# A fused attention and token-mixing kernel: w2 loaded in 11 pieces, matmul pairs with their own waits, all gate logits on VectorE, and another order of all tasks

## The chip, the core and the metric

The kernel runs on one core of a Trainium2 chip. The metric is the device time of one execution in microseconds (us), as the median of several runs. A core has five engines that run side by side, each through its own queue in order: PE (TensorE, matrix products into PSUM), ACT (ScalarE), DVE (VectorE), POOL (GpSimd) and SP (SyncE, which here only issues DMAs). They wait for each other through semaphores.

## What is computed

Two mixers work on the same x, of 2048 tokens by 512 features in bf16, and a gate mixes their results. A is attention with 32 heads of 16 features, in which a token sees itself and the 255 before it. B is a layer norm followed by a two-layer perceptron across tokens: its first product sums over the 2048 tokens (w1, 2048 x 1376), its second goes back to them (w2, 1376 x 2048).

```
g = sigmoid((x * gate_w).sum(-1))
a = softmax(mask(q @ k.T) * 16 ** -0.5) @ v @ wo       # q, k, v = x @ wqkv, per head
b = (gelu(layernorm(x).T @ w1 + b1) @ w2 + b2).T
out = g * a + (1 - g) * b
```

## The kernel before

Everything is resident in SBUF. Tokens are cut into 16 tiles of 128; group i means four tiles, 512 tokens. The program is a list of tasks, made by `add`. Each has a name, the engines that may do it, the tasks it depends on, and the buffers it takes. Two texts then fix the order: `PLAN` (from line 190) names for each engine the tasks in the order of its queue, with the numbers of the buffers each takes after the colon, and `THEN` names those attention tasks after which a plain matmul task is issued in column tiles. `arrange` (line 85) steps through these queues with estimated costs. It no longer chooses the order in a queue; it settles how the queues are interleaved when the program is written out, and which of the shared-port waits are set between VectorE and GpSimd. So `PLAN` and `THEN` set what runs; the costs in `arrange` served to search them.

The tasks that matter here, by name:

- `x0.0`, `x1.4` and so on: loads of x. `wqk0` to `wqk3`, `wv`: loads of wqkv. `xt1` to `xt3`: transposing loads of x by DMA (line 463); group 0 is transposed on TensorE (`xta`) and copied (`xtc`). `gw`: gate_w copied to all partitions. `w1_gi`: a quarter (512 tokens) of a group g of w1's columns. `w2_g`: w2, in the old kernel in 3 tasks of 4, 4 and 3 chunks of 128 rows. w2 lies in the same memory as w1, so a piece of it can be loaded only when the matmuls that read that part of w1 are done.
- `q`, `k`, `v`: projections, in chains of 4 matmuls (`chain`, line 653; its matmul is line 670). `qc`, `kc`, `vc` copy them out of PSUM. `vs` and `vz` move parts of V to other partitions by DMA (lines 718 to 729); `vz` has 3 buffers.
- For each block j of 128 queries, shifted by 64: `sj.v0` to `sj.v3` and `sj.C` are scores on TensorE (lines 942, 998, 1042); `e...` the exponentials on ScalarE (line 894); `m...` the masks, on VectorE (lines 907, 974) or GpSimd (line 536); `pvj` the products with V (line 1087); `n1j` to `n4j` and `nzj` the transposition and division on VectorE (lines 1178 to 1213). The result is put over x.
- `bs`, `ba`, `pow`, `h`: layer norm. `u0` to `u10`: 11 chains of 16 matmuls over tokens, one for 128 columns of w1; `ub` adds the bias; `gelu` acts on all of them.
- `gate0` with `gatem0`: gate logits of group 0 by 16 matmuls of one column (line 802); `gl4` to `gl15`: those of the other tiles on VectorE, one fused multiply-and-sum each (line 822). `gatee` and `ez` make the exponentials and spread them.
- `y0` to `y15`: for each output tile a chain of 11 matmuls with w2 and 4 with wo, in pairs; `f` scales and adds on the way out of PSUM (lines 438, 441), `o` stores (line 1305). `y15` is made in two halves of 256 columns, `y15l` and `y15r`.

A chain is issued in pieces of two matmuls, so that others can stand between; `u3.4` is the piece that begins with matmul 4. In the old kernel the first piece of a `u` chain waits for all four quarters of its group of w1 and all 16 `h`, and the first piece of a `y` chain for all of w2. TensorE has modes: plain 128 x 128 work ("d"), column tiles ("p"), scores ("s"), corners ("c", "h"). A change between them has a price, for which `arrange` has `SWITCH`. PSUM has 8 banks; a task on TensorE that takes a bank waits until the last reader of it is done.

Of the kernel before, what the change touches and what calls it, by code (L numbers as in the profile page):

```python
# [78 lines left out]
SWITCH = 0.095  # L79

BLOCK, AHEAD, FETCH, BUSY = 256, 80, 3.6, 3.0
LATENCY = {"PE": 0.22, "ACT": 0.15, "DVE": 0.12, "POOL": 0.15, "SP": 2.0}


def arrange(tasks):
# [19 lines left out]
    count, come, loads = AHEAD, {}, 0.0  # L105
    order = []
    while len(order) < len(tasks):
# [117 lines left out]
    ACT="""
        xtc0.0.1 xtc0.1.0 xtc0.1.1 kc3_0 kc1_0 kc0_0 kc2_0 e0.v0.0:4 e0.v0.1:5 kc3_1 e0.C.1:8 e0.C.0:a e-1.C.1:7
        e-1.C.0:b vc1 vc2 e1.v3.1:2 e1.v3.0:3 vc3 e1.v0.0:6 e1.v0.1:9 vc5 gatee0 e0.v1.0:d e0.v1.1:c vc14 kc2_1
        vc13 e1.v2.1:b e1.v2.0:7 vc12 vc15 kc2_2 e1.v1.0:5 e1.v1.1:a vc4 e2.v1.1:4 e2.v1.0:8 e1.C.1:d e1.C.0:c vc7
# [42 lines left out]
    """,  # L271
    SP="""
        x0.0 x0.2 wqk0 wqk1 wqk2 wqk3 x1.4 xt1 wv x2.8 bias xt3 x3.12 xt2 vs0 w1_02 w1_03 vs1 w1_22 vs2 gw w1_12
        w1_23 w1_01 w1_00 w1_10 w1_11 vz2:0 w1_13 vz3:1 vz4:2 vz5:0 w1_20 w1_21 vz6:1 vz8:0 w2_0 vz7:2 w2_1 w2_2
        vz9:1 wo o0 o4 o8 o7 vz10:2 vs13 o2 o9 o1 vz11:0 vz12:1 o5 o10 vz13:2 o11 vz14:0 o3 o6 o12 o14 o13 o15l
        o15r
    """,
# [1097 lines left out]
```

## Time and profile before

| | |
|---|---|
| Median of 3 runs | 199.59 us (198.86 to 199.63) |
| Profiled execution | 199.82 us, of which the span from first to last instruction is 198.1 |
| TensorE clock granted | 1.000 |
| Matmuls | 4058 |
| ACT, exponentials (lines with L894) | 89.3 + 58.1 us in two groups |
| GpSimd, masks (L536) | 46.7 + 20.0 us in two groups |
| DMA | 22.02 MB, 111 GB/s on average |

The page counts busy time for each engine, in total and in 40 slices, follows the chain of waits back from the end, and lists groups of instructions with their mean length and what ended the idle time ahead of them. Time is counted from the start of the span. The "end" of a matmul is modelled, so I go by starts: the next start less this one is what a matmul costs the stream. The DMA loads that matter:

```profile
wb<-in_B_w_dram SPq DMA_DIRECT2D x8, 512.0 KB, 8.2
wb<-in_B_w_dram SPq DMA_DIRECT2D x2, 2048.0 KB, 9.2
VZ<-VA SPq DMA_DIRECT2D x26, 70.0 KB, 3.0
xo<-in_A_x_dram SPq DMA_DIRECT2D x3, 512.0 KB, 5.5
```

The last number is the median from issue to landing in us. `wb` holds w1 and later w2.

### The profile page before, as it was taken

The numbers are of one execution on the slowest core, as the hardware profiler recorded it, in microseconds if no ns is written. First come the engines' busy times: TensorE is split into PE (matmuls) and PEld (weight loads), VectorE is DVE, ScalarE is ACT, GpSimd is POOL, SyncE is SP. The second block draws the span as 40 slices with busy tenths as digits, with TensorE's granted clock in tenths as the row PEclk, the third lists the DMA queues.
The fourth block names the chain that finished last, engine by engine and source line by source line (L and its number), as shares of the span: only waits on it lengthen the run. The fifth ranks groups of instructions, "written<-read, shape, count | busy, mean of one in ns | idle before, by whom it ended". The sixth has DMA issues, their size and how long they took to land. (4 is left out here: it accounts for less than half of the span.)

```text
span 198.1 us, 9100 instructions
## 1 busy us (share of the span) xinstructions
PE 193.0 (97%) x4058; PEld 93.3 (47%) x4058; DVE 156.5 (79%) x318; ACT 169.0 (85%) x198; POOL 80.0 (40%) x118
## 2 busy tenths in 40 slices
PE   7999999999999999999999999999999999999993
PEld 3643444353635445446543554344445354554572
DVE  1799888879998988986589799636867868869683
ACT  2369999999988996998999899899899989898632
POOL 6394897525344440214223200045069335452310
PEclk9999999999999999999999999999999999999999
DMA  5999798970060000001399770000211220200002
GB/s 156 294 284 232 131 319 278 346 187 0 8 174 18 18 0 3 3 5 32 98 364 367 280 210 3 26 26 30 68 37 58 60 68 22 62 30 30 30 3 83
DMA packets 23189, 22.02 MB, mean 111 GB/s; under 512 B 7566, under 2 KB 21262, under 8 KB 23150
## 3 DMA queue, kind: packets, MB, share of 16 engines
q1 hardware_dynamic: 23150, 21.44, 36.9%
q8 instruction: 32, 0.52, 1.1%
q14 instruction: 7, 0.06, 0.1%
HBM read 15.61 MB, written 2.10 MB: 89 GB/s over the span
## 5 line engine op out<-in xcount | busy, mean ns | idle before, releaser
L894 ACT ACTIVATE et<-ps 128x1024 bf16<-128x1024 f32 (+1 forms) x94 | 89.3, 1015 | 6.1 <-PE ps L942 2.4
L536 POOL TENSOR_SCALAR_AFFINE_SELECT et<-et 128x512 bf16<-128x512 bf16 (+2 forms) x63 | 46.7, 751 | 56.0 <-ACT et L894 40.9
L894 ACT ACTIVATE XT<-ps 128x1024 bf16<-128x1024 f32 (+1 forms) x60 | 58.1, 1011 | 7.3 <-PE ps L942 4.3
L670 PEld LDWEIGHTS <-wb 128*32 128x32 bf16 (+4 forms) x645 | 32.0, 97 | 34.5 <-issue 6.5
L670 PE MATMUL pb<-ug,wb 128*32 128x512 bf16 (+4 forms) x385 | 45.5, 366 | 0.0
L670 PE MATMUL pb<-h,wb 128*128 128x512 bf16 (+2 forms) x260 | 44.5, 381 | 0.0
L536 POOL TENSOR_SCALAR_AFFINE_SELECT XT<-XT 128x512 bf16<-128x512 bf16 (+1 forms) x28 | 20.0, 720 | 46.3 <-ACT XT L894 27.4
L670 PE MATMUL pb<-XT,wqkv 128*128 128x512 bf16 (+2 forms) x190 | 32.4, 372 | 0.4 <-DMA wqkv<-in_A_wqkv_dram 0.3
L1178 DVE STREAM_TRANSPOSE et<-ps 128x1024 f32<-128x1024 f32 (+1 forms) x17 | 20.1, 1183 | 11.9 <-PE ps L1087 11.1
L1087 PEld LDWEIGHTS <-VA 128*32 128x32 bf16 (+1 forms) x1056 | 20.1, 97 | 6.6 <-issue 1.5
L942 PE MATMUL ps<-QZ,KT 32*128 32x256 bf16 (+1 forms) x496 | 23.1, 265 | 0.0
L754 DVE TENSOR_TENSOR QZ<-pb,par 128x1024 bf16<-128x1024 f32 x16 | 19.5, 1221 | 3.2 <-PE pb L670 3.2
L670 PEld LDWEIGHTS <-wqkv 128*128 128x128 bf16 (+1 forms) x190 | 12.7, 98 | 14.6 <-DMA wqkv<-in_A_wqkv_dram 0.5
L670 PE MATMUL pb<-wo,xo 128*32 128x512 bf16 (+2 forms) x152 | 18.1, 375 | 0.0
L1087 PE MATMUL ps<-et,VA 128*32 128x128 bf16 (+2 forms) x624 | 17.9, 218 | 0.0
L942 PEld LDWEIGHTS <-KT 32*128 32x128 bf16 x496 | 7.4, 92 | 20.6 <-ACT et L894 10.7
L670 PE MATMUL pb<-wqkv,XT 128*128 128x512 bf16 (+1 forms) x70 | 16.5, 381 | 0.0
L974 DVE TENSOR_TENSOR et<-et,mask 128x512 bf16<-128x512 bf16 x26 | 13.3, 510 | 2.5 <-ACT et L894 2.4
L441 DVE TENSOR_SCALAR ot<-pb,c,c 128x512 bf16<-128x512 f32 (+1 forms) x11 | 8.6, 785 | 7.4 <-PE pb L670 7.3
L1087 PE MATMUL ps<-XT,VA 128*32 128x128 bf16 (+2 forms) x432 | 13.9, 215 | 0.0
L1087 PEld LDWEIGHTS <-VZ 128*32 128x32 bf16 x832 | 13.2, 98 | 0.7
L770 DVE BATCH_NORM_STATS2 stats<-xo 128x6 f32<-128x512 bf16 x16 | 10.7, 682 | 3.1 <-DMA xo<-in_A_x_dram 3.1
(76 smaller groups left out, 199.4 us busy)
## 6 DMA issues: line engine op xcount, KB each, us to landing
wb<-in_B_w_dram SPq DMA_DIRECT2D x8, 512.0 KB, 8.2
wb<-in_B_w_dram SPq DMA_DIRECT2D x2, 2048.0 KB, 9.2
VZ<-VA SPq DMA_DIRECT2D x26, 70.0 KB, 3.0
xo<-in_A_x_dram SPq DMA_DIRECT2D x3, 512.0 KB, 5.5
out_dram<-ot SPq DMA_DIRECT2D x12, 128.0 KB, 2.4
wb<-in_B_w_dram SPq DMA_DIRECT2D x4, 352.0 KB, 5.8
wqkv<-in_A_wqkv_dram SPq DMA_DIRECT2D x4, 256.0 KB, 5.0
wb<-in_B_w_dram SPq DMA_DIRECT2D x1, 1024.0 KB, 5.3
```

Of the source, the lines that this page charges most:

```text
L441: return nc.vector.tensor_scalar(out=out_, in0=in_, scalar1=scale, scalar2=bias, op0=ALU.mult, op1=ALU.add)
L536: return nc.gpsimd.affine_select(out=out_, in_=in_, pattern=[[0, n] for n in pattern] + [[step, HB]], compare_op=op, fill=0.0, base=base_, ...
L670: made.append(nc.tensor.matmul(buf(b)[c:z_, c0:c0 + w_], lhsT=lhsT[:, c:z_], rhs=rhs, start=(j == 0), stop=(j == n - 1), skip_group_check= ...
L754: lambda k=k, b=b: nc.vector.tensor_tensor(out=QZ[:, k, :, (i % NQ) * SB:(i % NQ + 1) * SB], in0=buf(b)[:, None, :].to_broadcast([P, 2, SB ...
L770: f"bs{t_}", {"DVE": 0.67}, lambda b=b, t_=t_: nc.vector.bn_stats(buf(b)[:], xo[:, t_, :]),
L894: lambda e=e, b=b, shape=shape: nc.scalar.activation(out=shape(buf(e)), in_=shape(buf(b)), func=ACT.Exp, scale=SCALE),
L942: made.append(nc.tensor.matmul(to[:, :, done:done + m], lhsT=keys(j if x == "A" else j - 1, k)[rows], rhs=q[rows], start=True, stop=True, ...
L974: made.append(nc.vector.tensor_tensor(out=v, in0=v, in1=m.to_broadcast(list(v.shape)), op=ALU.mult))
L1087: return lambda: nc.tensor.matmul(to(), lhsT=v() if callable(v) else v, rhs=buf(e)[rows, col:col + n], start=first, stop=last, tile_positi ...
L1178: lambda: nc.vector.transpose(out=view(buf(tr).bitcast(FP32)), in_=view(buf(o))), [last], takes=[tr], uses=[o],
```

## The change

It does five things.

1. `PLAN` and `THEN` are new for all engines. They were searched with other costs: a table `TURN` of the price of each change of mode, `cost_of` for tasks, other hand-over times, and a finer account of when TensorE's instructions are fetched and of loads that compete with it.
2. w2 is loaded in 11 pieces, one for each chunk of 128 rows (`w2_0` to `w2_10`), each waiting only for the u matmuls that read the part of w1 beneath it.
3. Pairs wait for their own pieces: in `u` for a quarter of w1 and one `h` per matmul, in `y` for one piece of w2.
4. `NGP = 0`: the logits of group 0 go to VectorE too (`gl0` to `gl3`), and `gate0` is gone.
5. `y15` is made in three parts, of 256, 128 and 128 columns (`y15l`, `y15m`, `y15r`). The zeros for the warm-up matmuls are 128 columns in place of 512 and read repeatedly.

Which engine does a task changes with `PLAN`: masks go from GpSimd to VectorE (GpSimd 82 to 67, VectorE 70 to 85). On VectorE `kc` goes from 7 to 5, `vc` from 2 to 5, `ub` from 7 to 5, `f` from 14 to 13, `xtc` from 1 to 2; ScalarE has the others.

```diff
-SWITCH = 0.095
-
-BLOCK, AHEAD, FETCH, BUSY = 256, 80, 3.6, 3.0
-LATENCY = {"PE": 0.22, "ACT": 0.15, "DVE": 0.12, "POOL": 0.15, "SP": 2.0}
+TURN = {
+    "d": dict(d=0, s=0.100, p=0.100, c=0.098, h=0.100),
...
+BLOCK, AHEAD, INSIDE, FETCH, BUSY = 256, 77, 194, 4.0, 2.4
+LATENCY = {"PE": 0.21, "ACT": 0.15, "DVE": 0.11, "POOL": 0.12, "SP": 2.3}
+
+
+def cost_of(t, e):
+    c, n = t.engines[e], t.name
+    if e == "PE":
+        return c - 0.02 if t.mode == "s" else c * 0.738 if t.mode == "c" else c
+    if e == "DVE":
+        return max(0.1, c - 0.06)
...
     SP="""
-        x0.0 x0.2 wqk0 wqk1 wqk2 wqk3 x1.4 xt1 wv x2.8 bias xt3 x3.12 xt2 vs0 w1_02 w1_03 vs1 w1_22 vs2 gw w1_12
-        w1_23 w1_01 w1_00 w1_10 w1_11 vz2:0 w1_13 vz3:1 vz4:2 vz5:0 w1_20 w1_21 vz6:1 vz8:0 w2_0 vz7:2 w2_1 w2_2
-        vz9:1 wo o0 o4 o8 o7 vz10:2 vs13 o2 o9 o1 vz11:0 vz12:1 o5 o10 vz13:2 o11 vz14:0 o3 o6 o12 o14 o13 o15l
-        o15r
+        x0.0 x0.2 wqk0 wqk1 wqk2 x1.4 wqk3 gw wv xt1 bias xt3 vs0 x2.8 vs1 xt2 w1_21 x3.12 w1_00 w1_01 w1_10
+        w1_02 w1_20 vs2 w1_23 w1_12 w1_11 vz4:1 w1_03 vz8:0 vz2:2 vz3:2 w1_13 w1_22 vz5:2 wo w2_0 w2_3 vz6:1
+        vz11:2 vz7:1 w2_1 w2_4 w2_2 w2_7 w2_6 w2_5 w2_8 vz10:0 w2_9 w2_10 vz9:1 o2 o4 o7 o0 o8 vz13:1 vz12:0
+        o5 o10 vs13 o1 o11 o9 vz14:1 o13 o3 o6 o12 o14 o15l o15r o15m
     """,
...
-    NGP = 1
+    NGP = 0
...
-    zeros = ug[:, 0, :]
+    zeros = ug[:, 0, 0:P]
...
-        b, t = chain(f"u{fc}", mms, dw1[g] + hready, "u")
+        b, t = chain(f"u{fc}", mms, [], "u", each=[[dw1[g][t_ // 4], hready[t_]] for t_ in range(NT)])
...
-    full_ = NFC - 1
-    for g in range(NG):
-        def emit(g=g):
-            lo, hi = 4 * g, min(4 * g + 4, full_)
-            nc.sync.dma_start(w2[:, lo:hi, :], B_w2[lo * P:hi * P, :].rearrange("(t p) s -> p t s", p=P))
-            if hi == full_:
-                nc.sync.dma_start(w2[:F - full_ * P, full_, :], B_w2[full_ * P:F, :])
-        dw2.append(add(f"w2_{g}", {"SP": 5.3 if g < 2 else 4.0}, emit, m1[4 * g:4 * g + 4], lat=2.5))
-
-
+    for fc in range(NFC):
+        g = fc // 4
+        fsz = min(P, F - fc * P)
+        row = min(NT - 1, ((fc - 4 * g + 1) * S - 1) // width[g])
+        gone = [piece[f"u{c}.{row // 2 * 2}"] for c in range(4 * g, min(4 * g + 4, NFC))]
+        dw2.append(add(
+            f"w2_{fc}", {"SP": 1.55 * fsz / P},
+            lambda fc=fc, fsz=fsz: nc.sync.dma_start(w2[:fsz, fc, :], B_w2[fc * P:fc * P + fsz, :]), gone, lat=2.9,
+        ))
...
-        parts = [("", 0, D)] if t_ < NT - 1 else [("l", 0, D // 2), ("r", D // 2, D)]
+        parts = [("", 0, D)] if t_ < NT - 1 else [("l", 0, D // 2), ("m", D // 2, 3 * D // 4), ("r", 3 * D // 4, D)]
...
-                f"y{t_}{tag}", mms, dw2, "y", tail=4,
+                f"y{t_}{tag}", mms, [], "y", tail=4, each=[[d] for d in dw2] + [[]] * 4,
```

The new orders of the engines, where the prediction speaks of them:

On TensorE (k3_2.0 is the first to read what `xt2` loads):

```
s0.v1:26 k3_1.0:4 k3_1.2 k3_2.0:5 s1.v2:06 k3_2.2
...
v9.0:3 v9.2 s2.v2:06 q2_1.0:5 k1_2.0:4 q2_1.2 s2.C:20
...
pv3.0:2 pv3.1 pv3.2 pv3.3 u3.0:7 u3.2 u3.4 s5.v2:04 u3.6 u3.8 u3.10 s4.v3:20
...
u4.12 q3_2.0:7 u4.14 pv4.0:4 pv4.1 pv4.2 pv4.3
...
y14.13 y15r.4 y15l.6 y15l.8 y15r.6 y15l.10 y15l.11 y15l.13
y15r.8 y15r.10 y15r.11 y15m.0:2 y15r.13 y15m.2 y15m.4 y15m.6 y15m.8 y15m.10 y15m.11 y15m.13
```

On VectorE:

```
vc9 h4 h11 m2.v0.1 h0 h9
...
n12:8 gl9 gl14 m3.v0.0
...
n13:a gl13 m4.v0.1
...
ub3 n32:1 m4.v0.0 n42 qc0_2 n31:1 m4.v2.0 gatem1 m4.C.1 m4.C.0 m4.v2.1
```

## The prediction

> **What bounds the kernel now.** I read the page from the top, then the 20 us stretches, then the chain of waits, then timelines of TensorE and VectorE.
>
> The page's first two parts, busy time by engine and in 40 slices:
>
> ```profile
> PE 193.0 (97%) x4058; PEld 93.3 (47%) x4058; DVE 156.5 (79%) x318; ACT 169.0 (85%) x198; POOL 80.0 (40%) x118
> ...
> PE   7999999999999999999999999999999999999993
> ```
>
> TensorE has a 9 in every slice but the first and the last. The same in stretches of 20 us (busy us of PE, PEld, DVE, ACT, POOL, each with its count; clock; DMA):
>
> ```profile
> 0.00:20.00 20.00, 18.27 (x136) 9.14 (x137) 14.11 (x31) 10.87 (x18) 11.87 (x25) 1.00 0.93 241
> ...
> 40.00:60.00 20.00, 20.00 (x443) 9.15 (x430) 18.13 (x39) 18.91 (x24) 7.92 (x10) 1.00 0.32 87
> 60.00:80.00 20.00, 20.00 (x438) 9.75 (x436) 17.50 (x40) 17.15 (x20) 7.64 (x13) 1.00 0.04 10
> ...
> 100.00:120.00 20.00, 19.82 (x421) 9.48 (x414) 17.50 (x37) 18.98 (x21) 3.87 (x6) 1.00 0.83 284
> ```
>
> From 20 to 100 us TensorE is never without a matmul. A busy TensorE can still be a slow one, so I price its stream from the chain of waits (start, length, what):
>
> ```profile
> 143.94 1.40 PE pb L670 x6
> ...
> 147.36 0.33 PE ps L942 x8
> 147.69 1.63 PE pb L670 x28
> 149.32 0.33 PE ps L942 x8
> ...
> 157.74 1.62 PE pb L670 x7
> ```
>
> Six full matmuls of 512 columns and one change of mode take 1.40 us, seven take 1.62: 0.22 each (0.216, when more of them are divided out) and 0.10 for the change. The same work cut into 28 column tiles takes 1.63, so the tiled form is neither cheaper nor dearer. A score task (x8) is 0.33 wherever nothing holds it up. On these prices nearly the whole stream runs without a wait. I find three real ones, together 0.45 us: the score task at 112.98 lasts until 113.56 (0.58, so 0.25 too long), 142.41 to 143.51 is 0.13 above its price, and 143.87 to 145.34 is 0.07 above. The first:
>
> ```profile
> 112.98 0.40 PE L942 MATMUL ps<-QZ,KT 32*128 32x256 bf16 x8
> 113.56 1.77 PE L670 MATMUL pb<-XT,wqkv 128*128 128x512 bf16 x7 [0.18 <-ACT XT L894]
> ```
>
> So the kernel is bound by TensorE's own stream of instructions. A new order can gain only what it takes out of the stream, these 0.45 us, and what lies at the two ends. It can lose as much as it makes TensorE wait.
>
> **What the Trainium skill says.** "TensorE: Matmul & The Clock Gate", section "Back-to-back issue gap", gives N/2.4 + 2.5 ns for a warm matmul, 216 at N = 512; the trace agrees (0.216). I use its 56 ns at N = 128 for the new 128-column outputs, which no warm row of the trace shows. The same page, "What's actually happening", says the clock is released by a free-running window of 3.4 us. In the trace the five warm-up matmuls take 0.43 us each and the projections reach full speed only at about 6.9 us, so a warm-up that begins 0.3 us earlier need not warm earlier: I give it nothing. "SBUF — State Buffer", section "SBUF: two separate sides", says that VectorE with two SBUF inputs and GpSimd lock each other out. The trace agrees: a VectorE mask of 512 columns takes 0.36 to 0.86 us.
>
> **TensorE, part by part.** The gate's matmuls go: gate0 starts at 23.02 and the next work at 23.43, so 0.41, of which the 16 matmuls are 0.40. In the new order of tasks I count 165 changes of mode for 169: 4 x 0.10 = 0.40. Summed task by task at the middle price of each kind, the two streams differ by 0.85: these two items and 0.05 of rounding. The last half row, 15 matmuls of 256 columns, becomes 30 of 128: 15 x 0.109 against 30 x 0.056, +0.03, within that rounding. Pairs that wait for their own piece of w1, h or w2 cost TensorE no instruction; they only let it be put earlier. **-0.85**.
>
> **Ends.** At the end VectorE's last output shrinks from 256 to 128 columns: 0.545 at 256 and 0.809 at 512 give 0.41 at 128, **-0.13**. The third output DMA goes out while TensorE works on the last 15 matmuls. At the start the projections wait until 6.57 for the first piece of wqkv, which stays third in SP's queue: 0.
>
> **w2 in 11 pieces.** Eleven DMAs for four, at 0.33 to 0.6 us of SP each, so 2 to 4 us more of a queue that is mostly empty after 65 us. The first two are now early, behind u3; most stand behind vz7, which waits for pv6 (stream position about 93.6), the last two behind vz10, which waits for pv8 (about 114.6). SP then needs 1.1 for vz10 and issues the last two at about 115.9 and 116.4; the 512 KB load of wo landed 5.4 after its issue behind a larger one, so they land by 121.3 and 121.8 at the worst; y0.8 and y0.10 stand at 121.2 and 121.7. Cost 0, bounds 0 and +0.5. The old order had its 4 MB burst in 96 to 115 us, and TensorE's stalls there name ScalarE, not a DMA: no gain.
>
> **VectorE.** This is where I expect the new wait. It takes over 4 gate logits (0.72 each) and 15 masks from GpSimd (85 for 70) and gives one evacuation to ScalarE, net; its tasks go from 275 to 293. Most of it falls early: up to the last mask of row block 4 the old queue holds 116 tasks, 60.6 us of work, the new one 132 tasks, 66.7 us. The prices are start to start in the timeline, where VectorE has no gap (masks 0.34, logits 0.72):
>
> ```profile
> 59.11 0.43 DVE L974 TENSOR_TENSOR XT<-XT,mask 128x512 bf16<-128x512 bf16 x1
> 59.45 0.68 DVE L822 SCALAR_TENSOR_TENSOR junk<-xo,gwr 128x512 bf16<-128x512 bf16 x1
> ...
> 61.61 0.68 DVE L822 SCALAR_TENSOR_TENSOR junk<-xo,gwr 128x512 bf16<-128x512 bf16 x1
> 62.21 0.08 DVE L822 DVE_READ_ACCUMULATOR junk<-xo,gwr 128x1 f32 x1
> 62.33 0.69 DVE L822 SCALAR_TENSOR_TENSOR junk<-xo,gwr 128x512 bf16<-128x512 bf16 x1
> ```
>
> The tight stretch runs from vc9 (free when v9 is done, position 42.6) to the last mask before pv4.2 (position 73.3). A position is 6.73, where the projections start with their half-speed ones allowed for, plus the prices of all TensorE tasks ahead; between these two stand 49 pairs of matmuls at 0.432, 11 score tasks, 3 corners, 10 parts of pv and 30 changes, 30.7 us. In it stand 58 VectorE tasks: 12 logits at 0.722, 14 masks at 0.335, 6 corner masks at 0.604, 10 h at 0.322, 2 qc at 1.141, 2 n1 at 1.174, 2 vc at 0.607, 10 others 4.0 together. Sum 30.0 us at the middle prices; at the mean prices (masks 0.41, corners 0.72, logits 0.69, port conflicts in them) 31.9. With 0.2 us of hand-over at each end VectorE is between 0.3 early and 1.6 late, and what it is late TensorE waits, because pv3, ub3, ub4 and pv4 stand behind it in turn. GpSimd has 15 tasks fewer, so fewer conflicts: I take **+0.35**, bounds 0 and +1.6. In the old order VectorE was idle for 1.87 and 2.50 us of the two stretches from 40 to 80 us shown above.
>
> **Other hand-overs.** The old 0.45 of waits go with the old order; I put as much in for those of the new one, bounds -0.45 and +0.5. ScalarE gets about 1.4 us more work (two evacuations of K, two of u and two outputs more, three of V and one of XT less) and stays near 87%.
>
> **SP's early queue.** xt2 moves behind vs0, x2.8 and vs1, and vs0 waits for vc0. Before, xt2 was issued at 16.6. Now: xt1 at about 5.3 and held 5.7 to 6.5, bias 1.4, xt3 3.2 to 4.3, then 2.8: xt2 at 19.2 to 20.3, landing 6.4 later (median of the transposes), 25.6 to 26.7. Its first reader k3_2.0 stands at 26.8. Cost 0, bounds 0 and +1.0.
>
> **Sum.** -0.85 - 0.13 + 0.35 = -0.63. The profiled execution took 199.82 (span 198.1 and 1.7 around it), 0.23 above the median 199.59: it becomes 199.2, the median 198.95, which I give as 199.0.
>
> **Rivals.**
> - A clean order (chance 0.30): VectorE keeps its middle prices and most of the old 0.45 is gone. -0.98 - 0.4 = 198.2. For it: a sum of 30.0 fits in 30.7. Against it: no slack is left in it.
> - VectorE becomes the bound from 43 to 73 us (0.18): mean prices, +1.4 in place of 0.35, 200.0; at 5% above them 201. It decides from 0.543 us for a mean task of that stretch (0.517 at middle prices, 0.550 at mean ones): then its lateness exceeds 0.98, and the change is a loss. For it: VectorE at 18.13 of 20 in the old order already. Against it: fewer GpSimd masks.
> - SP's queue is late (0.10): XT2 lands 1 us after its reader is due, and the last pieces of w2 come late as well: 199.59 - 0.98 + 1.3 = 199.9. The piecewise waiting then does nothing for the end, since the stream has no wait on w2 to remove.
>
> **How the numbers follow.** The forecast has 0.42, its own range 198.4 to 199.5. About 0.5% (1.0 us) is what a measurement of this kernel tells from no change: faster is under 198.6, slower over 200.6. Faster: the clean order 0.30 and a part of the forecast 0.10. Slower: the upper half of the VectorE case 0.08 and the worst of SP's 0.03. The rest, 0.49, is the same. Range 197.9 to 200.5, from a clean order with nothing new in it to VectorE at its mean prices with an SP delay.
>
> **What would show it.** The gate's row at L802 gone; TensorE's sum of stretches near 192.2 where nothing new waits; VectorE at 19 of 20 or more in 40 to 80 us, and TensorE waits that name VectorE at pv3, pv4 or a u chain there (none: the clean order; over 1 us: the second rival); a wait on XT at 26 to 28 us or on wb after 120 for the third. I am wrong if TensorE shows waits of over 1 us anywhere else, or if a change of mode costs other than 0.10.

## The result, and the profile after

| | before | after |
|---|---|---|
| Median (20 runs each, taken together) | 200.06 us (198.86 to 201.03) | 199.59 us (199.12 to 200.28) |
| Ratio of after to before | | 0.9975, 95% interval 0.9963 to 0.9987 |
| Profiled execution, and its span | 199.82 us, 198.1 | 199.20 us, 197.5 |
| Last matmul ends | 195.00 us | 194.59 us |
| Clock | 1.000 | 1.000 |

The change gains 0.25%, 0.47 us between the medians. The forecast gave the profiled execution 199.2 and got that. It took the level of the medians, though, from three runs of the kernel before, whose median (199.59) lies 0.47 us under that of twenty.

To see where time went I walk along TensorE's queue and compare the start of each task with the sum of the middle prices of all tasks ahead of it. The difference is what TensorE has lost so far by waiting, or by starting late. The "repeat" is the changed kernel once more, another execution.

| Lost by TensorE, us | first score task | at 45 us | at 110 us | at 150 us | at the end |
|---|---|---|---|---|---|
| before | 1.97 | 2.05 | 2.55 | 3.27 | 3.46 |
| after | 1.42 | 2.18 | 2.48 | 3.63 | 3.89 |
| repeat of after | 1.75 | 2.17 | 2.47 | 3.62 | 3.88 |

The queue's own work falls by 0.84 (191.38 to 190.54), the losses rise by 0.43, and what follows the last matmul shrinks from 3.1 to 2.9 us. That is the 0.6 us of span.

The page's busy time of the engines, and TensorE's slices:

```profile
PE 187.4 (95%) x4008; PEld 92.3 (47%) x4040; DVE 157.8 (80%) x340; ACT 169.9 (86%) x200; POOL 64.6 (33%) x102
...
PE   7999999999999999999999999899999999999994
```

The trace lacks 32 records of matmuls (4008 of 4040; the weight loads, PEld, are complete), so this busy time is too low. The one "8" in the row, 123.4 to 128.4 us, lacks three of them and also holds real waits, shown below. VectorE is 1.3 us busier, GpSimd 15.4 us less. In stretches of 20 us I read the repeat instead, which has all records (columns as before):

```profile
40.00:60.00 20.00, 19.80 (x379) 8.89 (x370) 19.62 (x48) 18.54 (x23) 5.27 (x9) 1.00 0.30 77
60.00:80.00 20.00, 20.00 (x480) 9.47 (x479) 18.01 (x38) 17.98 (x22) 4.96 (x8) 1.00 0.33 109
120.00:140.00 20.00, 19.62 (x326) 8.43 (x325) 13.53 (x32) 19.39 (x22) 3.87 (x6) 1.00 0.18 54
```

VectorE has 19.62 of 20 us from 40 to 60, as feared, yet TensorE is short of only 0.20 us there, and of nothing from 60 to 80. The gap that the prediction didn't have is at 120 to 140. TensorE's weight loads there, in the changed kernel's first trace (start, length, what, and in brackets the idle time ahead and what ended it):

```profile
122.97 0.10 PEld L708 LDWEIGHTS <-wb 96*128 96x128 bf16 x1 [0.44 <-DMA wb<-in_B_w_dram]
123.74 0.12 PEld L980 LDWEIGHTS <-KT 32*128 32x128 bf16 x8 [0.67 <-ACT et L932]
...
125.57 0.12 PEld L980 LDWEIGHTS <-KT 32*128 32x128 bf16 x8 [0.53 <-ACT et L932]
```

The first is y0.10, which waits for the eleventh piece of w2, landed at 122.93. The other two are the score tasks s9.v3 and s9.v2, which wait for a bank that ScalarE has yet to read. A score task has some 0.42 us of idle weight loading ahead of it when nothing is late, so the excess counts: against the prices these three lose 0.12, 0.46 and 0.11 us, and pv8.0 and s10.v2 another 0.24. The eleventh piece went out late: SyncE issued vz10 at 116.00 and the last two pieces of w2 (`wb`) behind it.

```profile
116.00 0.47 SPq L766 DMA_DIRECT2D VZ<-VA  x1
116.56 0.55 SPq L767 DMA_DIRECT2D VZ<-VA  x1
117.16 1.07 SPq L1315 DMA_DIRECT2D wb<-in_B_w_dram  x2
```

ScalarE in the same time:

```profile
114.89 1.28 ACT L1291 ACT_TABLE_LOAD   x1
116.18 4.66 ACT L1291 ACTIVATE ug<-ug 128x1536 bf16<-128x1536 bf16 x3
...
121.37 1.28 ACT L932 ACT_TABLE_LOAD   x1
122.67 2.85 ACT L932 ACTIVATE et<-ps 128x1024 bf16<-128x1024 f32 x3
```

From 114.89 to 122.67 it makes no exponential: the gelu, with an exchange of tables on each side. The Trainium skill, "ScalarE: Activation LUTs", section "What ACT_TABLE_LOAD costs", gives about 1283 ns for one; the trace agrees with 1.28 us.

### The profile page after: what moved, and what is told of

The parts are those of the page before. It is cut to its first block, busy times and chain, and to the rows that moved or that the text cites. A ratio compares the mean times of both kernels' runs of the same rounds, so it can differ in the third digit from the quotient of the medians.

```text
span 197.5 us, 9026 instructions
## 1 busy us (share of the span) xinstructions
PE 187.4 (95%) x4008; PEld 92.3 (47%) x4040; DVE 157.8 (80%) x340; ACT 169.9 (86%) x200; POOL 64.6 (33%) x102
## 4 chain that ended last, share of the span: by engine, by line
PE 79%; ACT 11%; DVE 4%; issue 3%; DMA 2%; SPq 0%; ACTq 0%
PE pb L708 57%; PE ps L1125 10%; PE ps L980 9%; ACT et L932 7%; PE ps L1080 2%; ACT VA L640 2%; DMA wqkv<-in_A_wqkv_dram 2%; DVE stats L808 1%; ACT L932 1%; DVE et L1216 1%; DVE zt L1233 0%; SPq L489 0%; ACT ug L1291 0%; DVE h L824 0%; PE ps L1036 0%
## 5 line engine op out<-in xcount | busy, mean ns | idle before, releaser
L932 ACT ACTIVATE et<-ps 128x1024 bf16<-128x1024 f32 (+1 forms) x104 | 98.8, 1011 | 8.2 <-PE ps L980 5.5
L571 POOL TENSOR_SCALAR_AFFINE_SELECT et<-et 128x512 bf16<-128x512 bf16 (+3 forms) x60 | 41.6, 704 | 98.4 <-ACT et L932 65.7
L932 ACT ACTIVATE XT<-ps 128x1024 bf16<-128x1024 f32 (+1 forms) x50 | 49.1, 1028 | 1.2 <-PE ps L980 0.7
L708 PE MATMUL pb<-ug,wb 128*32 128x512 bf16 (+6 forms) x344 | 43.9, 365 | 0.9 <-issue 0.6
L708 PE MATMUL pb<-h,wb 128*32 128x512 bf16 (+2 forms) x301 | 41.9, 380 | 1.7 <-issue 1.7
L1216 DVE STREAM_TRANSPOSE et<-ps 128x1024 f32<-128x1024 f32 (+1 forms) x13 | 15.7, 1207 | 4.2 <-PE ps L1125 3.7
L571 POOL TENSOR_SCALAR_AFFINE_SELECT XT<-XT 128x512 bf16<-128x512 bf16 (+1 forms) x15 | 9.8, 659 | 24.5 <-ACT XT L932 13.5
L708 PE MATMUL pb<-wo,xo 128*32 128x512 bf16 (+3 forms) x152 | 17.5, 369 | 0.4 <-issue 0.3
L708 PE MATMUL pb<-wqkv,XT 128*128 128x512 bf16 x60 | 15.8, 380 | 0.6 <-issue 0.3
L1012 DVE TENSOR_TENSOR XT<-XT,mask 128x512 bf16<-128x512 bf16 x20 | 9.7, 485 | 6.4 <-ACT XT L932 6.4
```

Of the source, the lines that this page charges most:

```text
L571: return nc.gpsimd.affine_select(out=out_, in_=in_, pattern=[[0, n] for n in pattern] + [[step, HB]], compare_op=op, fill=0.0, base=base_, ...
L708: made.append(nc.tensor.matmul(buf(b)[c:z_, c0:c0 + w_], lhsT=lhsT[:, c:z_], rhs=rhs, start=(j == 0), stop=(j == n - 1), skip_group_check= ...
L932: lambda e=e, b=b, shape=shape: nc.scalar.activation(out=shape(buf(e)), in_=shape(buf(b)), func=ACT.Exp, scale=SCALE),
L1012: made.append(nc.vector.tensor_tensor(out=v, in0=v, in1=m.to_broadcast(list(v.shape)), op=ALU.mult))
L1216: lambda: nc.vector.transpose(out=view(buf(tr).bitcast(FP32)), in_=view(buf(o))), [last], takes=[tr], uses=[o],
```

## The experiments

All ratios are to the kernel before, in runs on the same chip; the changed kernel's is 0.9975 (0.9963 to 0.9987).

| kernel | median us (runs) | ratio, 95% interval | lost from 110 to 150 us |
|---|---|---|---|
| a_same (repeat) | 199.35 (9) | 0.9976 (0.9956 to 0.9995) | 1.15 |
| a_ywhole | 199.65 (12) | 0.9993 (0.9965 to 1.0021) | |
| a_early | 199.17 (22) | 0.9964 (0.9948 to 0.9980) | 1.19 |
| a_s9 | 200.09 (21) | 1.0004 (0.9982 to 1.0025) | 1.32 |
| a_nogelu (gelu left out) | 199.87 (14) | 0.9995 (0.9974 to 1.0016) | 1.14 |
| a_w2early | 199.69 (22) | 0.9974 (0.9958 to 0.9990) | 1.12 |
| a_w2s9 | 200.47 (22) | 1.0003 (0.9983 to 1.0022) | 1.31 |
| a_three | 200.32 (14) | 0.9996 (0.9973 to 1.0020) | 1.34 |
| a_w2nogelu (gelu left out) | 199.03 (6) | 0.9933 (0.9914 to 0.9951) | 0.38 |
| a_wqk3 | 200.36 (22) | 1.0012 (0.9996 to 1.0029) | 1.12 |
| a_wqk3e | 200.26 (22) | 0.9993 (0.9973 to 1.0013) | |
| a_gate | 203.27 (6) | 1.0142 (1.0113 to 1.0171) | |
| b_start | 200.25 (22) | 1.0010 (0.9995 to 1.0024) | |
| b_gate | 204.94 (6) | 1.0246 (1.0220 to 1.0272) | |
| b_w2 | 203.62 (6) | 1.0176 (1.0142 to 1.0209) | |
| b_w2late | 200.54 (22) | 1.0012 (0.9995 to 1.0029) | 0.70 |

Names with a_ begin from the changed kernel, those with b_ from the kernel before, which itself loses 0.72 us from 110 to 150.

**The change as it is, twice.** a_same is unchanged.

> The changed kernel once more, as it is. Accounting of the two traces, task by task: TensorE's stream is 1.0 us shorter than before, the first matmul is 0.34 us earlier, and waits new to this order give back 0.93 us; net -0.4 at TensorE's end and -0.6 in the span. If that is the kernel and not the one execution, the ratio to the kernel before is again 0.996 to 0.999, the first projection again starts at 5.8 to 5.9 us, and the score tasks s9.v3 and s9.v2 again wait about 0.4 and 0.1 us for ScalarE near 124 and 125.6 us. Rival (the early start is the chance of one execution): the first projection starts anywhere from 5.8 to 6.6 us and the ratio moves by up to 0.003 with it.

Ratio 0.9976; s9.v3 and s9.v2 lose 0.20 and 0.10, and y0.10 now 0.38 rather than 0.12, since its piece lands at 123.18. The sum of the three is the same (0.69 and 0.68). The early start was chance in part (1.75 lost at the first score task, not 1.42), and by 45 us nothing is left of the difference.

```diff
-                f"y{t_}{tag}", mms, [], "y", tail=4, each=[[d] for d in dw2] + [[]] * 4,
+                f"y{t_}{tag}", mms, dw2, "y", tail=4,
```

> The changed kernel, in which each y chain's first pair waits for all 11 pieces of w2, as in the kernel before. Theory (waiting by pieces is what permits the new order): the first y task, y4.0, stands at about 118.9 us and then waits for the last piece, which lands at 122.9; all of TensorE is 3.5 to 4.5 us later, less what the later waits for ScalarE (0.69 us) then hide: 2.8 to 4.5 us slower than the changed kernel, ratio to the kernel before 1.012 to 1.021. Rival (the pieces land early enough that the grain of the wait does not matter, as I took for the time in my sum): within 0.5 us of the changed kernel.

A miss, with a plain cause: the instructions and waits of all five queues come out the same as without the edit. The waits of the program follow from the data that each instruction reads; `each` tells only `arrange` what a task must wait for. So for the y chains the third item of the change moves no wait by itself, and what is said above of the first piece of a chain, that it waits for all of w2, holds for `arrange` only. The same item in the u chains was not run alone. What the item did was let the search put y4.0 ahead of the last pieces, and TensorE again waits for the eleventh piece alone, at y0.10. As a third set of runs of the changed kernel it shows how wide one set can lie.

**The waits near 123 us.** Six kernels. First the score tasks later:

```diff
-        y0.8 y0.10 s9.v3:40 y0.11 y0.13 y4.8 s9.v2:02 y4.10 y4.11 y2.0:7
+        y0.8 y4.8 y0.10 y0.11 s9.v3:40 y0.13 y4.10 y4.11 s9.v2:02 y2.0:7
```

> Only TensorE's order near 123 us differs: the two score tasks s9.v3 and s9.v2 come two pairs of matmuls later, and the pair y4.8 comes ahead of y0.10. Theory (the 0.69 us lost between 119 and 128 us is a wait of TensorE that another order covers: 0.12 for the eleventh piece of w2 and 0.57 for banks that ScalarE's exponentials free after the gelu): these waits fall to under 0.15 together, ScalarE gets its scores just in time, and the kernel is 0.4 to 0.6 us faster than the changed one, a ratio of 0.9945 to 0.996 to the kernel before. Rival (ScalarE bounds this stretch, so that its delay returns): the waits near 124 go, but as much comes back at the score tasks and pv products from 127 to 145 us; time as the changed kernel, ratio 0.997 to 0.998.

The rival's mechanism, at a ratio above its range. The waits at s9.v3 and s9.v2 go, y0.10 loses 0.21, and s9.C loses 0.53 at 127.99, waiting for a bank that ScalarE reads until 127.94. Then ScalarE's work left out:

```diff
-        made = [nc.scalar.activation(ug[:, a:z, :], ug[:, a:z, :], ACT.Gelu_apprx_tanh) for a, z in cuts]
+        made = [nc.scalar.activation(ug[:, a:z, :], ug[:, a:z, :], ACT.Identity) for a, z in cuts]
```

> The gelu is left out: its four instructions on ScalarE copy instead, over the same elements, so that no activation table is exchanged (1.28 us each time). Theory (the gelu with its two tables makes the 0.57 us that TensorE waits for ScalarE near 124 us): ScalarE is through about 2.6 us earlier, those waits go, 0.12 for the last piece of w2 stays or grows, since TensorE comes to it earlier; 0.4 to 0.6 us faster than the changed kernel, ratio to the kernel before 0.9945 to 0.996. Rival (the waits come from the distance between the scores and the banks, whatever ScalarE did before): they stay at 0.4 us or more, ratio 0.9965 to 0.998. If the 2.6 us of ScalarE matter later too, the ratio falls below 0.994.

No table is exchanged now, the score tasks near 125 us wait for nothing, and it is no faster. TensorE's weight loads:

```profile
124.65 0.10 PEld L708 LDWEIGHTS <-wb 96*128 96x128 bf16 x1 [1.08 <-DMA wb<-in_B_w_dram]
124.97 0.12 PEld L980 LDWEIGHTS <-KT 32*128 32x128 bf16 x8 [0.23 <-issue]
```

The eleventh piece takes the whole loss: 0.75 us at y0.10. Now that piece earlier, with the gelu in:

```diff
-        vz11:2 vz7:1 w2_1 w2_4 w2_2 w2_7 w2_6 w2_5 w2_8 vz10:0 w2_9 w2_10 vz9:1 o2 o4 o7 o0 o8 vz13:1 vz12:0
+        vz11:2 vz7:1 w2_1 w2_4 w2_2 w2_7 w2_6 w2_5 w2_8 w2_9 w2_10 vz10:0 vz9:1 o2 o4 o7 o0 o8 vz13:1 vz12:0
```

> The changed kernel with the last two pieces of w2 ahead of vz10 in SP's queue. In five traces of the changed order TensorE waits 0.12 to 0.78 us at y0.10 for the eleventh piece, issued at 117.8 to 118.8 behind vz10, which waits for pv8. Theory (two things are late at the same time near 123.5 us, the piece and the banks that ScalarE frees): the pieces are issued by 113.5 and land by 119, the wait at y0.10 goes, and the wait at the next score task, s9.v3, becomes 0.4 to 0.8 us instead; loss between 119 and 128 us still 0.5 to 0.7 us, time within 0.2 us of the changed kernel. Rival (the piece is the cause alone, ScalarE's wait only follows it): the loss falls under 0.3 and the kernel is 0.4 us faster.

As the theory has it. The last piece lands at 117.19 and y0.10 doesn't wait, but s9.v3 does, with ScalarE's name and 0.58 us against its price:

```profile
125.03 0.12 PEld L980 LDWEIGHTS <-KT 32*128 32x128 bf16 x8 [1.00 <-ACT et L932]
```

With both taken away:

> The gelu is left out as before (copies over the same elements, no exchange of tables), and the last two pieces of w2 are ahead of vz10. Each alone left 0.7 to 0.9 us lost between 119 and 140 us. Theory (two things are late there by about the same amount, so either alone hides the other): with both gone the loss between 119 and 140 us falls from 0.87 to under 0.3 us, and the time to 0.4 to 0.7 us under the changed kernel's, ratio 0.993 to 0.996, if the start is like the changed kernel's median. Rival (something else holds TensorE there, as the bank chain of the score tasks alone): loss still 0.6 us or more.

```profile
120.94 2.26 PEld L708 LDWEIGHTS <-wb 128*128 128x128 bf16 x11
123.62 0.12 PEld L980 LDWEIGHTS <-KT 32*128 32x128 bf16 x8 [0.43 <-issue]
...
125.35 0.12 PEld L980 LDWEIGHTS <-KT 32*128 32x128 bf16 x8 [0.42 <-ACT et L932]
```

No load waits longer than an undisturbed one. The loss from 110 to 150 us falls from 1.15 to 0.38, and the ratio to 0.9933, whose interval lies wholly under the changed kernel's. (The changed kernel was not run again beside it; its program, run three times, gave 0.9975, 0.9976 and 0.9993, and none of these intervals reaches below 0.9956.) So two things are late at 123 us, by nearly the same amount. Either one removed alone leaves the time as it was.

Could an order with the gelu do as well? The seven score tasks from s9.v3 to s11.v3 were put later, the first two by a pair and a half and the others by one pair (less than the expectation says), on top of the early pieces, and then the moved masks (below) were added:

> As the one with the early pieces, and all six score tasks from s9.v3 to s11.v3 come one and a half to two pairs of y matmuls later, at the same distance from each other as before, so that none of them asks for a bank before ScalarE gives it. Theory (both late things are now covered): loss between 119 and 128 us under 0.25 us, no wait on ScalarE at s9.C as when two score tasks were moved alone, 0.4 to 0.6 us faster than the changed kernel, ratio to the kernel before 0.994 to 0.996. Rival (ScalarE bounds the stretch to 160 us, so the wait moves on): at s10 to s12 or pv9 to pv11 as much is lost, ratio 0.997 to 0.999.

> The early pieces, the later score tasks and the two moved masks together. If each removes its own waits: losses of about 0.35 us at 30 to 45 us and 0.5 at 119 to 128 us gone, 0.7 to 1.0 us faster than the changed kernel, ratio to the kernel before 0.9925 to 0.9945. Rival (what is won early only makes a later wait longer, since the later one is set by ScalarE's own chain): no better than the one with the score tasks alone.

Not with these two. In both the loss from 120 to 130 us falls, to 0.2 and 0.3, and s10.v2 and pv9.0, behind the shifted stretch, lose 0.36 and 0.11 to ScalarE, which is busy 19.3 of 20 us there. Near the end pv15.1 loses another 0.3 in both. Here the shift of a few tasks gave the wait to the first ones that weren't shifted. The edit also has a cost of its own: y2.0 takes the bank of y0 and now follows it more closely, and y7.0 takes that of y4, whose copy f4 stands on VectorE behind the mask of a shifted score task. They lose 0.19 and 0.29 us in one trace, 0.21 and 0.10 in the other. An order without that, or one shifted up to 160 us, was not tried.

**VectorE and GpSimd at 30 to 43 us.** The changed kernel on VectorE (first trace), and the score task s2.v2 on TensorE in the repeat:

```profile
38.37 0.69 DVE L641 CAST KT<-pb 128x512 bf16<-128x512 f32 x1 [1.00 <-PE pb L708]
...
39.57 0.88 DVE L945 TENSOR_TENSOR XT<-XT,mask 128x512 bf16<-128x512 bf16 x1
...
41.42 1.25 DVE L1216 STREAM_TRANSPOSE et<-ps 128x1024 f32<-128x1024 f32 x1
```

```profile
42.80 0.40 PE L980 MATMUL ps<-QZ,KT 32*128 32x256 bf16 x8 [0.16 <-ACT et L932]
```

VectorE idles for 1.00 us ahead of kc0_1 while the mask m1.C.0 stands behind it. The mask holds up pv1.4 (0.12 lost), and with it the transpose n11, which ends at 42.65. s2.v2 needs its bank and loses 0.23. The view names ScalarE as the releaser, but its last reading of these banks had ended at 41.79: VectorE was the later one.

```diff
-        ... ba12 bs15:1 kc0_1 bs14:0 m1.C.0 ba14
+        ... ba12 bs15:1 m1.C.0 kc0_1 bs14:0 ba14
-        ... m0.C.1 pow1 m1.v3.1 m0.C.0 m0.v1.0 m0.v1.1 m1.v0.1
+        ... m0.C.1 pow1 m0.C.0 m0.v1.0 m0.v1.1 m1.v3.1 m1.v0.1
```

> Two masks are moved within their own queues: m1.C.0 on VectorE ahead of the copy kc0_1, into a gap of 1.0 us at 37.4 us, and m1.v3.1 on GpSimd behind m0.v1.1. Theory (the waits at pv0.2, s2.v1, pv1.4 and s2.v2 between 30 and 43 us, 0.72 us together, come from the order within VectorE's and GpSimd's queues): they fall to 0.1 to 0.3 together, and the kernel is 0.3 to 0.6 us faster than the changed one, ratio to the kernel before 0.9945 to 0.9965. Rival (VectorE has no slack in 40 to 60 us, 19.64 of 20 us busy, so what is won early is lost at the next thing it makes TensorE wait for): ratio 0.997 to 0.998, with new waits on VectorE between 43 and 75 us.

The mask now runs in the gap, and the transpose starts 0.31 us sooner:

```profile
37.42 0.48 DVE L944 TENSOR_TENSOR XT<-XT,mask 128x512 bf16<-128x512 bf16 x1
38.42 0.69 DVE L640 CAST KT<-pb 128x512 bf16<-128x512 f32 x1 [0.53 <-PE pb L707]
...
41.11 1.25 DVE L1215 STREAM_TRANSPOSE et<-ps 128x1024 f32<-128x1024 f32 x1 [0.23 <-ACT KT L639]
```

The loss from the first score task to 45 us is 0.12 in place of 0.42 in the repeat (0.76 in the first trace, where pv0.2 and s2.v1 lose 0.21 and 0.16 as well), and no new wait on VectorE follows up to 75 us. But y0.10, reached 0.1 us earlier than in the repeat, then waits 0.78 us for its piece of w2, which lands 0.3 us later. What reaches the end is little: 0.9964 against 0.9975, intervals that overlap. It is the best of these kernels that computes everything, and is not shown to beat the changed one.

**The gate's matmuls.** In the kernel before, gate0 was taken out (`NGP = 0`), gl0 to gl3 were put on VectorE and gw moved ahead of x1.4:

```diff
-    NGP = 1
+    NGP = 0
-        ... ba9 bs11:1 biasc vc0 bs5:0 ba11 ba5 bs10:1 bs7:0 ba10 ba7 gatem0 bs14:1
+        ... ba9 bs11:1 gl0 gl1 biasc vc0 bs5:0 ba11 ba5 bs10:1 bs7:0 ba10 ba7 gl2 gl3 gatem0 bs14:1
```

> The kernel before with the gate's 16 matmuls and their task gone; the logits of group 0 are four fused multiply-and-sums more on VectorE near 20 us, and gate_w is loaded ahead of x1.4. Theory (the 0.41 us leave TensorE's stream and VectorE has room for 2.9 us in its first 20 us): 0.2 to 0.4 us faster than the kernel before, ratio 0.998 to 0.999. Rival (VectorE is late by the 2.9 us, with q copies and masks behind it, from 20 us on, as the new waits from 30 to 43 us of the changed kernel hint): no gain or up to 1 us slower, ratio 1.000 to 1.005, with TensorE waits on VectorE between 20 and 45 us.

The rival, and five times what it allowed. TensorE in the stretch (releaser in the brackets):

```profile
20.74 1.90 PE L670 MATMUL pb<-wqkv,XT 128*128 128x512 bf16 x8 [0.96 <-DVE QZ L754]
...
23.12 0.60 PE L670 MATMUL pb<-XT,wqkv 128*128 128x512 bf16 x2 [0.48 <-DVE gwc L563]
```

By 30 us it has lost 5.5 us (1.9 before), and later shifts bring a further stop of 1.0 us at 98.7. In the other direction, gate0 back into the changed kernel behind q1_1.2 and gl0 to gl3 out:

> The changed kernel with group 0's gate logits back on TensorE: 16 matmuls of one column behind q1_1.2, and four multiply-and-sums fewer on VectorE ahead of 22 us. Theory (my prediction's term): TensorE's stream is 0.40 us longer, and VectorE's 2.9 us early were free or nearly so; 0.2 to 0.4 us slower than the changed kernel, ratio to the kernel before 0.9985 to 0.9995. Rival (VectorE's late tasks at 30 to 43 us, 0.35 us at pv1.4 and s2.v2, come from those 2.9 us): these waits go with them and the time is within 0.1 us of the changed kernel or under it. Second rival (32 more instructions move the places where TensorE's queue is refilled): a stop inside a task that no trace of the changed order has.

Slower as well, by 1.7%: 2.2 us are lost from 18 to 24 us (1.28 where v14.0 waits for the DMA of XT, 0.94 where gate0 waits for ScalarE to free its bank), and score task s5.v2 stops for 1.17 us within itself, as the second rival said. The wait at v14.0 need not come from the edit: a_w2early, which has the changed kernel's order there, loses 0.95 us at the same place. Both directions lose. The 0.4 us are out of TensorE's stream, but no run isolates what that alone is worth.

**w2 in 11 pieces alone**, in the kernel before:

```diff
-        ... vz8:0 w2_0 vz7:2 w2_1 w2_2 vz9:1
+        ... vz8:0 w2_0 w2_1 w2_2 w2_3 vz7:2 w2_4 w2_5 w2_6 w2_7 w2_8 w2_9 w2_10 vz9:1
```

with items 2 and 3 of the change.

> The kernel before, with w2 in 11 pieces put where its three loads stood, and pairs that wait for their own pieces; the order of every other queue is as it was. Theory (the pieces bring nothing by themselves, since the old order has no wait on w2): within 0.2 us of the kernel before, ratio 0.999 to 1.001. Rival (smaller, earlier pieces change what SP's queue does: more issues ahead of vz7 delay it, or the wait of TensorE at 113 us or 146 us is one on a DMA under ScalarE's name): 0.2 to 0.5 us either way.

Neither: 1.8% slower. The largest stop of TensorE, 2.3 us, is inside task u4.4, with no semaphore to wait for, and SyncE's issues stand ahead of it:

```profile
97.10 0.40 PE L669 MATMUL pb<-h,wb 128*32 128x512 bf16 x4
99.63 0.40 PE L669 MATMUL pb<-h,wb 128*32 128x512 bf16 x4 [2.14 <-issue]
```

```profile
92.71 3.62 SPq L1276 DMA_DIRECT2D wb<-in_B_w_dram  x4
...
97.60 1.11 SPq L1276 DMA_DIRECT2D wb<-in_B_w_dram  x1
```

The trace also records the packets that carry instructions: 32 in this program, on a DMA queue of their own. In the kernel before, the thirteenth starts at 94.77 us; here, with TensorE's queue up to that point within 0.05 us of it, it starts at 97.39 and ends at 98.34, behind four pieces of 512 KB. (In the kernel before, nothing of w2 is on the way at 94.77: its first load is issued at 96.04.) TensorE goes on 1.3 us later. The Trainium skill, "Runtime: NRT & Kernel Launch", section "Instruction fetch mechanics", says that instructions come in blocks of 256 through a DMA queue of the sequencer's own, and that this is mostly hidden. The number of packets agrees (the trace of the kernel before has 8157 records of TensorE, 31.9 blocks). Mostly hidden it is, but not here. To test it, the pieces stand behind vz7:

> The kernel before with w2 in 11 pieces as in the slow one, but all of them behind vz7 in SP's queue, so that the first is issued at about 97.5 rather than 92.7 us. In the slow one TensorE stops for 2.3 us at 97.1 in the middle of a task, with nothing it waits for, and the instruction packet that starts at 94.8 us in the kernel before starts only at 97.4, behind the first pieces. Theory (the pieces are in the way of TensorE's own instruction fetch): the packet starts by 95 us, the stop is gone, ratio 0.998 to 1.004. Rival (the 11 pieces cost SP and the stream as such): ratio over 1.012 again.

The pieces now start at 93.43 rather than 92.71, the packet gets in at 94.56 and ends at 96.12, and of the stop of 2.3 us 0.32 is left, for 0.7 us of delay. The next packet is late in turn (102.60 to 103.56, for 101.09 in the kernel before) and brings a stop of 0.63:

```profile
97.47 0.10 PEld L669 LDWEIGHTS <-wb 128*32 128x32 bf16 x3 [0.42 <-issue]
...
105.04 0.19 PEld L1041 LDWEIGHTS <-KT 32*64 32x64 bf16 x17 [0.55 <-issue]
```

The time is that of the kernel before. The same kind of stop, 1.3 to 1.5 us after a packet's end, is in b_gate (packet's end 97.43, next load 98.69) and a_gate (65.85, 67.38).

**The start.** In the kernel before, the new zeros and warm-up alone:

> The kernel before with the start of the changed one alone: zeros of 128 columns, set ahead of the constants, and read repeatedly by the warm-up matmuls. Theory (the clock of TensorE starts to rise from its first work, so that a start 0.34 us earlier also gives full speed earlier, and the projections lose less at half speed): the first projection starts at 5.9 to 6.2 us rather than 6.57, the loss by the first score task falls from 1.97 us by 0.3 to 0.5, ratio 0.9975 to 0.9985. Rival (my prediction's: the first piece of wqkv, third in SP's queue, sets the start, and the earlier warm-up gives nothing): first projection at 6.4 to 6.7, ratio 0.9995 to 1.0005.

In its trace the loss at the first score task is 1.48 rather than 1.97, as the theory has it, but the time isn't shorter, as the rival has it: 0.8 us are lost again after 165 us. Most of it are two stops inside tasks s13.v2 and s14.C, of the same kind again: the instruction packets ahead of them end at 170.66 and 179.22.

```profile
172.05 0.09 PEld L945 LDWEIGHTS <-KT 32*128 32x128 bf16 x1 [0.25 <-issue]
...
180.67 0.11 PEld L1045 LDWEIGHTS <-KT 32*64 32x64 bf16 x4 [0.39 <-issue]
```

b_w2 stops at the same two places, for 0.33 and 0.43 us. What made these packets late was not looked for. And in the changed kernel, the fourth piece of wqkv back ahead of x1.4, without and with the two moved masks:

> The changed kernel with the fourth piece of wqkv ahead of x1.4 in SP's queue, as in the kernel before. In nine traces of the changed order TensorE has lost 1.4 to 3.6 us (median 2.05) by the first score task, in five of the order before 1.5 to 2.1 (median 1.94), and in the changed order a projection waits 0.2 to 1.0 us for the piece that lands at 9.6 to 11.2 us. Theory (the order of those two loads costs the new start 0.2 to 0.4 us on average): no projection waits for the fourth piece, the loss by s0.v0 is 1.2 to 1.8 us, the kernel is 0.1 to 0.4 us faster than the changed one, ratio to the kernel before 0.9955 to 0.997. Rival (the start is absorbed: TensorE then waits at v1.0 for wv, or between 30 and 45 us for VectorE, as the changed kernel's own repeat shows, 1.75 and 1.42 us at s0.v0 but 2.17 and 2.18 at 45 us): ratio 0.997 to 0.998, loss at 45 us still 2.1 or more.

> The same with the two masks moved as well (m1.C.0 on VectorE, m1.v3.1 on GpSimd), so that the waits at 30 to 43 us, in which an earlier start could vanish, are gone. Theory: loss at 45 us 1.4 to 1.9 us rather than 2.2, and this is not all given back near 123 us; ratio to the kernel before 0.9935 to 0.996. Rival (the pieces of w2 and ScalarE's chain near 123 us take back what is won ahead of them): ratio 0.9965 to 0.9975.

Slower than the changed kernel, or no faster, which neither theory nor rival had. In a_wqk3 no matmul waits for the fourth piece, but x1.4 now comes later, VectorE waits for it with the copies of q behind it, and the first score task waits 0.70 us for these. VectorE in a_wqk3 and in the changed kernel:

```profile
10.30 1.29 DVE L808 BATCH_NORM_STATS2 stats<-xo 128x6 f32<-128x512 bf16 x2 [2.37 <-DMA xo<-in_A_x_dram]
```

```profile
9.12 1.29 DVE L808 BATCH_NORM_STATS2 stats<-xo 128x6 f32<-128x512 bf16 x2 [1.49 <-DMA xo<-in_A_x_dram]
```

## Why the prediction was right or wrong

The kernel was forecast at 199.0 and took 199.59. The step that failed for this number is its base: the median of three runs was taken for the level of the kernel before, and it lies 0.47 us under that of twenty. The sum of the changes came out, but in part by luck: three of its terms failed, the wait of VectorE (+0.35 where nothing new was lost), the other hand-overs (0 where 0.4 was lost) and the landing of w2. Term by term:

- **The stream, -0.85.** Right: -0.84 at the middle prices. Its largest item, the gate, couldn't be shown alone. The matmuls of 128 columns cost 0.056 each in the new traces, as taken. The page that this comes from, in the Trainium skill "TensorE: Matmul & The Clock Gate", section "Back-to-back issue gap", gives its formula for an isolated matmul; here it fits the stream, with 0.216 and 0.056. In the sum, 30 of them against 15 at 0.109 are +0.045 and not +0.03, which changes nothing.
- **The end, -0.13.** Right in sign, measured -0.2: the time from last matmul to end is 2.88 to 3.01 us in the traces of the changed order and 3.09 to 3.16 in the others. VectorE's last output takes 0.41 us, as estimated.
- **The start, 0.** Right by result. The first trace starts 0.55 us better, but the lost time at the first score task lies at 1.4 to 3.6 us (median 2.05) in eleven traces of the new start and at 1.65 to 1.97 in three of the old, and part of an early start is gone by 45 us.
- **VectorE at 43 to 73 us, +0.35.** This step failed: VectorE is as full as the sum has it (19.62 of 20 us), and yet from 45 to 70 us TensorE loses only 0.12 (0.28 before). There are 0.35 us at pv1.4 and s2.v2, 40 to 43 us; that the size fits is chance, since they come not from the sum of VectorE's work, which I had added up, but from one task behind a waiting one. I had looked for the tight stretch by sums only. (The sums also count 0.4 us of hand-over for "1.6 late" and 0.2 for the rival's +1.4 and its 0.543.)
- **Other hand-overs, 0.** The old waits went, as I said: 0.53 by this measure. I put as much in for new ones. From 110 to 150 us alone they are 0.93, so the term is mis-sized by 0.4 or more. What is behind it is the piece of w2 and the banks that ScalarE frees after the gelu, both due near 123 us: with both taken away 0.38 is lost in that stretch and not 1.15.
- **w2 in 11 pieces, 0, landed by 121.8 at the worst.** This step failed. It let vz10 go where pv8 stands in the queue, at 114.6. But a buffer is free when the last part has read it: pv8.3 ends at 115.98, vz10 goes out at 116.00, the last two pieces at 117.2 and 117.8, and they land at 121.4 and 122.9. y0.10 waits 0.12 to 0.78 us in the traces with that order of loads. Putting the pieces earlier alone gains nothing (0.9974), and that is a second miss: ScalarE is late there as well, after a gelu that the search cost at 7.0 us and that takes 7.8 from the table to the first exponential. I had read "ScalarE stays near 87%" as room.
- **SP's early queue, 0.** Right: XT2 lands at 24.67, ahead of 26.8.
- **The level.** The change of the profiled execution was forecast at -0.63 us and measured at -0.62. Set against the twenty runs before, 0.25% is 0.5 us (0.26 to 0.74), and the sum lies in that interval. The stated 199.0 is 0.6 too low because its base, the median of three runs, was 0.5 too low; the 0.1 left is within the interval. That the sum fits so well is luck: it has +0.35 for losses, all of them on VectorE from 43 to 73 us, and the first traces differ by +0.43, of which -0.55 fall up to the first score task, +0.68 from there to 45 us, -0.20 up to 110, +0.43 up to 150 and +0.07 after.

Of the rivals, the clean order fell to the waits near 123 us and VectorE as the bound fell in its stretch. The third had its place right for w2 (a wait on wb after 120 us) and not for XT2.

## What to carry to other kernels

When a wait is removed and the time stays, look for a second one due at the same moment, and remove both: here either alone gave nothing, and both gave 0.4%. In a queue that runs without gaps, take the end of the last reader for the moment at which a buffer is free, and check each in-order queue for a ready task behind a waiting one, which no sum of busy time shows. A part of a jointly searched order, put alone into another, tells little of its worth: the gate's change alone cost 2.5% one way and 1.7% the other, the 11 pieces alone 1.8%.

## What the runs showed of the hardware

- A burst of loads can stop TensorE with no semaphore involved: an instruction packet that starts 2.6 us late behind 2 MB of loads costs 2.3 us, and moving the burst by 0.7 us, behind vz7, leaves 0.3 us of the stop. One profiled execution of each shows this; the times of their other runs agree (203.62 and 200.54 us).
- TensorE resumes 1.3 to 1.5 us after such a packet's record ends (98.34 to 99.63, 96.12 to 97.47, 97.43 to 98.69, 65.85 to 67.38, 179.22 to 180.67).
- Programs with the same start lose between 1.4 and 3.6 us before their first score task, from one profiled execution to the next. In the slowest (a_w2s9) matmuls of 256 columns still took 0.213 us each at 9.6 us, twice the 0.109 of later ones.
